# Two rules for dealing out feed-forward matmuls beside a top-k attention on one core

## The chip, the core and the metric

The kernel runs on one NeuronCore of a Trainium2 chip, as one program. The metric is the device time of that program in microseconds (us), the median of three runs. The core has five engines with an instruction stream each: TensorE (PE in the profile; its weight loads are PEld), VectorE (DVE), ScalarE (ACT), GpSimd (POOL) and SyncE (SP), which here issues the transfers.

## The reference

Attention with a top-k mask over 8 batches of 8 heads, 576 tokens and 64 elements a head, and then a gated feed-forward block over all 4608 tokens:

```python
scores = scale * np.matmul(q, k.transpose(0, 1, 3, 2))
kth = np.partition(scores, -32, axis=-1)[..., -32:-31]
scores = np.where(scores >= kth, scores, -1000000000.0)
attn = softmax(scores)                    # with 1e-9 added to the sum
x = attn @ v                              # as (4608, 512), heads side by side
out = (silu(x @ w_gate) * (x @ w_val)) @ w_out   # 512 -> 1536 -> 512
```

All inputs and outputs are float32.

## The kernel before

**Units.** The attention is cut into 160 units `(b, qt, hp)`: 8 batches, five tiles of queries, four pairs of heads. Within a batch the first 16 units hold 128 queries of two heads (double units, two rows of 576 scores for each partition); the last four, `qt == J`, hold the 64 left-over queries of both heads stacked in one tile (single units, one row). Unit 20b + 4qt + hp is the one with these three numbers, so units 16 to 19, 36 to 39, and so on are single.

**Stages of a unit.** TensorE makes the scores (L306, or L292 for a single unit) and ScalarE copies them out of PSUM (L311, L297). VectorE then finds the 32nd largest score of each row: four rounds of an eight-value maximum (L327) with three match-and-replace passes between (L331), and a comparison (L337). GpSimd adds the mask to the scores (`penalize`, L349). ScalarE takes the exponential and its sum (`weigh`, L358), VectorE the reciprocal (L370), and ScalarE scales (`normalize`, L373). TensorE transposes the weights (`turn`, L385; ScalarE copies them out, L386) and multiplies by v (`values`, L405 and L414; ScalarE copies the result into `xT`, L429). `prep` (L246) transposes k and q of a pair of heads once for each batch, on TensorE.

**The order of work.** There is no run-time scheduler: the main loop (L694) writes all instructions in order, and every engine keeps that order (the manual dependencies from L757 on see to it). Iteration n deals with several units at once: the top-k of unit n, the scores of n + 1, the penalty and exponential of n - 1, the scaling of n - 2, `turn` of n - 3, `values` of n - 4, and `prep` for unit n + 2 where that unit starts a pair. On TensorE an iteration is thus: turn, values, scores of the next unit, and then pieces of the feed-forward block.

**Pieces.** The feed-forward block works on 18 blocks of 256 tokens. `feed` (L454) is a generator that issues one block's matmuls in small steps and says what each one cost. A product of the gate or the value weights is two pieces of four matmuls, each of cost 1; there are twelve products, so 24 pieces. The down projection is seven quarter products of six matmuls, in pieces of three matmuls, each of cost 0.75: 14 pieces, 10.5 in sum. A block costs 34.5; the first, which is computed plainly, 36. A finished product puts its ScalarE work on a list, `on_act` (three instructions for a gate, L493 to L495; one copy for a value, L500), and GpSimd's work on `on_pool`; both are written into the streams at fixed places of the iteration (`flush`).

**Credit.** How many pieces an iteration may issue is set by `credit`. Each iteration adds 4.45 for a double unit and 2.25 for a single one, up to 8 (L714). `pieces(k)` (L667) issues up to k pieces as long as at least 1 is left, and an iteration calls it four times: 2 before the list for ScalarE is flushed and the scaling is written, then 1, 1 and up to 6. A block can begin only when `values` has filled all its tokens (`done`, L647); while none is ready, nothing is issued and the credit stays, up to 8. From unit 156 on the credit is 8 each time (L711). What is left after the loop is issued in one go (L751).

Of the kernel before, what the change touches and what calls it, by code (L numbers as in the profile page):

```python
# [27 lines left out]
def kernel(  # L28
# [40 lines left out]
    J = S // P  # L69
# [64 lines left out]
    def weights():  # L134
# [6 lines left out]
        for c in range(MC):  # L141
            for f in range(0, DM, WP):
                pieces.append((w_out[c * P : (c + 1) * P, f : f + WP], wo[:, c, f : f + WP]))
        pieces = [rounded(*p) for p in pieces]
        step = [0] * len(pieces)

        def upto(i, k):
# [51 lines left out]
    def rounding(n):  # L199
        for _ in range(n):  # L200
            next(weight, None)
# [9 lines left out]
    def load(i):  # L211
        b, hp = pairs[i]
        h = slice(2 * hp, 2 * hp + 2)
        kq = ld.tile([P, 2, J, 2, D], FP32, tag="kq", name="kq_in")
        kq_last = ld.tile([P, 2, D], FP32, tag="kql", name="kq_last")
        for n, src in ((0, k), (1, q)):
            queue = nc.scalar if n == 1 and i == 0 else nc.sync
            for hh in range(2):
                queue.dma_start(
                    kq[:, n, :, hh, :],  # L220
                    src[b, 2 * hp + hh, 0:JP].rearrange("(p j) d -> p j d", j=J),
                )
            queue.dma_start(
                kq_last[n * R : (n + 1) * R], src[b, h, JP:S].rearrange("h p d -> p h d")
            )
        raw[i] = (kq, kq_last)
# [42 lines left out]
    units = [(b, qt, hp) for b in range(B) for qt in range(J + 1) for hp in range(NHP)]  # L269
    state = {}  # L270

    def n_heads(qt):

        return 1 if qt == J else 2

    def scores(n):
        b, qt, hp = units[n]
        slab = preps[b * NHP + hp]
        sc = work.tile([P, 2 * S], FP32, tag="sc", name="sc", bufs=2)
        halves = [slice(0, D), slice(D, P)]  # L280
        half = S // 2

        def bank():
            return ps_t.tile([P, 512], FP32, tag="t", name="s")


        if qt == J:
            banks = [bank() for _ in range(2)]
            for i, ps in enumerate(banks):
                for d in halves:  # L290
                    k0 = R + i * half
                    nc.tensor.matmul(  # L292
                        ps[d, 0:half], slab[d, S + R : S + 2 * R], slab[d, k0 : k0 + half]
                    )
            yield
            for i, ps in enumerate(banks):
                nc.scalar.copy(sc[:, i * half : (i + 1) * half], ps[:, 0:half])  # L297
        else:
            q0 = S + 2 * R + qt * P
            banks = []  # L300
            for i in range(2):
                for hh, d in enumerate(halves):
                    ps = bank()
                    banks.append((i + 2 * hh, ps))
                    k0 = (1 - hh) * R + i * half
                    nc.tensor.matmul(  # L306
                        ps[:, 0:half], slab[d, q0 : q0 + P], slab[d, k0 : k0 + half]
                    )
            yield
            for i, ps in banks:  # L310
                nc.scalar.copy(sc[:, i * half : (i + 1) * half], ps[:, 0:half])  # L311
        state[n] = dict(sc=sc)

    def select(n):

        nh = n_heads(units[n][1])
        sc = state[n]["sc"]
        m = small.tile([P, 2, TOP_K], FP32, tag="m", name="m", bufs=2)
        heads = [slice(t * S, (t + 1) * S) for t in range(nh)]
        rest = work.tile([P, 2 * S], FP32, tag="rest", name="rest", bufs=1)  # L320
        e = work.tile([P, 2 * S], FP32, tag="e", name="e", bufs=4)
        state[n] |= dict(m=m, e=e, heads=heads)
        cur = sc
        rounds = TOP_K // 8
        for r in range(rounds):
            for t, hs in enumerate(heads):
                nc.vector.max(m[:, t, 8 * r : 8 * r + 8], cur[:, hs])  # L327
                yield
            if r < rounds - 1:
                for t, hs in enumerate(heads):  # L330
                    nc.vector.match_replace(  # L331
                        rest[:, hs], m[:, t, 8 * r : 8 * r + 8], cur[:, hs], LOWEST
                    )
                    yield
                cur = rest
        for t, hs in enumerate(heads):
            nc.vector.tensor_scalar(  # L337
                e[:, hs], sc[:, hs], m[:, t, TOP_K - 1 : TOP_K], FAR, ALU.is_lt, ALU.mult
            )

    def penalize(n):

        st = state[n]
        sc, m, e, heads = st.pop("sc"), st.pop("m"), st["e"], st["heads"]
        nh = len(heads)
        bias = small.tile([P, 2], FP32, tag="bias", name="bias")
        nc.gpsimd.tensor_scalar_mul(bias[:, 0:nh], m[:, 0:nh, 0], -scale)
        every = slice(0, nh * S)
        nc.gpsimd.tensor_tensor(e[:, every], e[:, every], sc[:, every], ALU.add)  # L349
        st["bias"] = bias  # L350
# [15 lines left out]
    def normalize(n):  # L366
        st = state[n]
        tot, e, heads = st.pop("tot"), st["e"], st.pop("heads")
        nh = len(heads)
        nc.vector.reciprocal(tot[:, 0:nh], tot[:, 0:nh])  # L370
        yield
        for t, hs in enumerate(heads):
            nc.scalar.mul(e[:, hs], e[:, hs], tot[:, t : t + 1])  # L373
# [76 lines left out]
    def flush(queue):  # L450
        while queue:
            queue.pop(0)()
# [186 lines left out]
    def piece():  # L639

        if len(on_act) > 1:
            flush(on_act)
        if len(on_pool) > 1:
            flush(on_pool)
        while True:
            if not current:
                if not todo or done.get(todo[0], 0) < NHP * BLK:  # L647
                    return 0
                flush(on_act)
                flush(on_pool)  # L650
                current.append(feed(todo.pop(0)))
            cost = next(current[0], 0)
            if cost == 0:
                current.pop()
                continue
            return cost

    def fetch(n):

        b, qt, hp = units[n]  # L660
        i = b * NHP + hp
        if qt == 0:
            yield from prep(i)
        if qt == J and i + NHP < len(pairs):
            load(i + NHP)

    def pieces(n):  # L667
        for _ in range(n):
            if credit[0] >= 1:
                credit[0] -= piece()  # L670

    def run(steps):
        for _ in steps:
            pass

    def finish_unit(n):
        values(n)
        b, qt, hp = units[n]
        if qt == J and b + 1 < B:
            load_v((b + 1) * NHP + hp)  # L680
# [8 lines left out]
    credit = [0.0]  # L689
    no = iter(())  # L690
    over = {}
    TURN, VALUES = 3, 4
    due = [0.0]
    for n in range(NU + VALUES):  # L694
        nh = n_heads(units[n][1]) if n < NU else 1
        topk = select(n) if n < NU else no
        over[n - 1] = normalize(n - 1) if 0 <= n - 1 < NU else no
        nxt = scores(n + 1) if n + 1 < NU else no
        ahead = fetch(n + 2) if n + 2 < NU else no
        norm = over.pop(n - 2, no)  # L700

        def dve(k, beside=True):

            for _ in range(k * nh):
                next(topk, None)
                due[0] += 5 / 11 if beside else 0
                if due[0] >= 1:
                    due[0] -= 1
                    rounding(1)

        if n >= NU - NHP:  # L711
            credit[0] = 8.0
        else:
            credit[0] = min(credit[0] + (4.45 if nh == 2 else 2.25), 8.0)  # L714
        flush(on_act)
        if 0 <= n - 1 < NU:
            penalize(n - 1)
        flush(on_pool)
        if 0 <= n - TURN < NU:
            run(turn(n - TURN))  # L720
        if n >= VALUES:
            finish_unit(n - VALUES)
        next(nxt, None)

        early[0]()
        if 0 <= n - 1 < NU:
            weigh(n - 1)
        run(nxt)

        dve(2, beside=False)  # L730
        if 2 <= n + 2 < NHP:
            load(n + 2)
        if n < NHP:
            load_v(n)
        pieces(2)
        flush(on_act)
        dve(1)
        dve(1)
        next(norm, None)
        run(norm)  # L740

        flush(on_pool)
        next(ahead, None)
        pieces(1)
        next(ahead, None)
        dve(1)
        pieces(1)
        dve(2)
        run(topk)
        pieces(6)  # L750
# [50 lines left out]
```

## Time and profile before

| | before |
|---|---|
| runs, us | 1870.55, 1870.92, 1871.88 |
| span of the profiled execution, us | 1870.2 |
| mean granted TensorE clock | 0.957 |
| PE busy, us (share) | 1715.9 (92%) |
| DVE busy, us (share) | 1632.2 (87%) |
| ACT busy, us (share) | 1210.1 (65%) |
| POOL busy, us (share) | 1023.4 (55%) |
| moved between HBM and core | 59.67 MB, mean 32 GB/s |

How to read it: busy time is summed over the whole span, start and end included. The ends of matmuls are modelled in the profile, so a busy PE says that it had something in hand, and not that it ran at its full rate. The page also cuts the span into 40 slices of 46.8 us and gives the busy share of each in tenths. A wait is put down to the instruction whose semaphore came last.

### The profile page before, as it was taken

Reading aid. Unit: us, or ns where it says so; the run is one execution under the profiler, and the core shown is the slowest. Engines: PE = TensorE matmul, PEld = TensorE weight load, DVE = VectorE, ACT = ScalarE, POOL = GpSimd, SP = SyncE. Lnnn points to the kernel's source line nnn. Section 1 sums busy time; section 2 is a strip of 40 time slices with the busy share of each in tenths; the row PEclk is TensorE's granted clock in tenths of the full one; section 3 lists DMA queues with packets and bytes.
Section 4 is the critical chain, followed back from the end, with each engine's and each line's share of the span. In section 5 each row is a group of like instructions: output and inputs, shape, how many; then the busy total and the mean of one; then the engine's idle time right before and its main releaser. Section 6 shows DMA issues by size and latency. Waiting matters only on the chain.

```text
span 1870.2 us, 30845 instructions
## 1 busy us (share of the span) xinstructions
PE 1715.9 (92%) x10756; PEld 1415.0 (76%) x10756; DVE 1632.2 (87%) x3477; ACT 1210.1 (65%) x3015; POOL 1023.4 (55%) x1007
## 2 busy tenths in 40 slices
PE   3447899899999999898999999989999999899998
PEld 2336658778888878787788887878888878787877
DVE  7999999998999989997999989999999989999300
ACT  5667667666757676765666676667666667676431
POOL 4666755645465646454455555555456545455534
PEclk7668999999999999999999999999999999999989
DMA  7332121000300021000200002000200001000000
GB/s 188 96 85 80 64 65 26 12 1 8 84 1 12 1 60 32 12 1 13 71 20 1 12 16 76 1 12 2 70 21 13 1 17 50 12 1 12 1 12 12
DMA packets 111259, 59.67 MB, mean 32 GB/s; under 512 B 89088, under 2 KB 97280, under 8 KB 111104
## 3 DMA queue, kind: packets, MB, share of 16 engines
q1 hardware_dynamic: 109904, 57.41, 11.6%
q8 instruction: 85, 1.39, 0.3%
q14 instruction: 70, 0.57, 0.1%
q10 hardware_dynamic: 1200, 0.30, 0.1%
HBM read 48.23 MB, written 9.44 MB: 31 GB/s over the span
## 4 chain that ended last, share of the span: by engine, by line
PE 80%; DVE 7%; ACT 4%; POOL 3%; issue 2%; DMA 0%; POOLq 0%; ACTq 0%; SPq 0%
PE f L468 39%; PE x_ps L554 8%; PE av L414 8%; PE etps L385 8%; PE s L306 6%; PE y_ps L554 5%; DVE m L327 3%; DVE rest L331 2%; PE s L292 2%; PE av L405 1%; ACT e L358 1%; PE kqps L261 1%; PE o_ps L514 1%; POOL e L349 1%; ACT sc L311 1%
## 5 line engine op out<-in xcount | busy, mean ns | idle before, releaser
L327 DVE MAX8 m<-rest 128x8 f32<-128x576 f32 x864 | 615.0, 746 | 2.2
L331 DVE MATCH_REPLACE8 rest<-m,rest 128x576 f32<-128x576 f32 x576 | 423.7, 742 | 0.0
L349 POOL TENSOR_TENSOR e<-e,sc 128x1152 f32<-128x1152 f32 (+1 forms) x160 | 382.7, 2392 | 59.5 <-DVE e L337 56.8
L468 PE MATMUL f<-xT,wg 128*128 128x256 f32 x1728 | 403.8, 384 | 0.0
L468 PE MATMUL f<-xT,wv 128*128 128x256 f32 x1728 | 397.9, 381 | 0.0
L468 PEld LDWEIGHTS f<-xT,wg 128*128 128x128 f32 x1728 | 323.7, 191 | 66.2 <-issue 23.9
L468 PEld LDWEIGHTS f<-xT,wv 128*128 128x128 f32 x1728 | 324.4, 190 | 55.6 <-issue 13.5
L496 POOL TENSOR_TENSOR h<-h,half_g 128x512 f32<-128x512 f32 x108 | 137.9, 1276 | 372.3 <-ACT h L495 360.6
L327 DVE MAX8 m<-sc 128x8 f32<-128x576 f32 x288 | 205.3, 749 | 122.7 <-ACT sc L297 71.1
L385 PE MATMUL etps<-ident,e 128*128 128x128 f32 (+1 forms) x1312 | 191.0, 291 | 122.3 <-issue 38.5
L358 ACT ACTIVATE e<-e,bias 128x576 f32<-128x576 f32 x288 | 222.0, 776 | 94.3 <-POOL e L349 94.3
L385 PEld LDWEIGHTS etps<-ident,e 128*128 128x128 f32 (+1 forms) x1312 | 161.9, 150 | 153.6 <-issue 45.4
L386 ACT COPY et<-etps 128x512 f32<-128x512 f32 (+1 forms) x448 | 185.1, 484 | 127.1 <-PE etps L385 125.6
L501 POOL TENSOR_TENSOR h<-h,val 128x512 f32<-128x512 f32 x108 | 139.4, 1291 | 159.4 <-ACT val L500 159.4
L373 ACT ACTIVATE e<-e,tot 128x576 f32<-128x576 f32 x288 | 211.6, 788 | 5.6 <-DVE tot L370 5.6
L331 DVE MATCH_REPLACE8 rest<-m,sc 128x576 f32<-128x576 f32 x288 | 211.8, 742 | 0.0
L414 PE MATMUL av<-et,v 128*64 128x128 f32 (+1 forms) x2560 | 175.7, 284 | 0.0
L337 DVE TENSOR_SCALAR e<-sc,m 128x576 f32<-128x576 f32 x288 | 172.6, 636 | 3.4
L306 PE MATMUL s<-kqT 64*128 64x288 f32 x1024 | 169.8, 447 | 4.2 <-ACT kqT L266 3.8
L311 ACT COPY sc<-s 128x288 f32<-128x288 f32 x512 | 163.8, 403 | 1.7 <-PE s L306 1.7
L493 ACT ACTIVATE h<-f 128x512 f32<-128x512 f32 x108 | 65.2, 604 | 150.7 <-PE f L468 150.7
L414 PEld LDWEIGHTS av<-et,v 128*64 128x64 f32 x2560 | 138.6, 146 | 23.4 <-issue 7.7
(71 smaller groups left out, 2042.0 us busy)
## 6 DMA issues: line engine op xcount, KB each, us to landing
kq_in<-in_k_dram SPq DMA_DIRECT2D x64, 128.0 KB, 2.8
v<-in_v_dram SPq DMA_DIRECT2D x32, 256.0 KB, 2.9
kq_in<-in_q_dram SPq DMA_DIRECT2D x62, 128.0 KB, 2.9
w<-in_moe_w_gate_dram SPq DMA_DIRECT2D x24, 256.0 KB, 2.7
w<-in_moe_w_val_dram SPq DMA_DIRECT2D x24, 256.0 KB, 2.7
w<-in_moe_w_out_dram SPq DMA_DIRECT2D x24, 256.0 KB, 2.6
out_dram<-o SPq DMA_DIRECT2D x40, 128.0 KB, 2.4
out_dram<-o SPq DMA_DIRECT2D x16, 256.0 KB, 2.4
```

Source lines behind the costliest of these rows:

```text
L306: nc.tensor.matmul(ps[:, 0:half], slab[d, q0 : q0 + P], slab[d, k0 : k0 + half])
L311: nc.scalar.copy(sc[:, i * half : (i + 1) * half], ps[:, 0:half])
L327: nc.vector.max(m[:, t, 8 * r : 8 * r + 8], cur[:, hs])
L331: nc.vector.match_replace(rest[:, hs], m[:, t, 8 * r : 8 * r + 8], cur[:, hs], LOWEST)
L349: nc.gpsimd.tensor_tensor(e[:, every], e[:, every], sc[:, every], ALU.add)
L358: nc.scalar.activation(e[:, hs], e[:, hs], AF.Exp, bias=bias[:, t : t + 1], scale=scale, accum_out=tot[:, t : t + 1],)
L373: nc.scalar.mul(e[:, hs], e[:, hs], tot[:, t : t + 1])
L385: nc.tensor.transpose(ps[0:kl, c * P : (c + 1) * P], e[:, k0 : k0 + kl], ident[:])
L386: nc.scalar.copy(et[0:kl, c0 : c0 + cn, :], ps[0:kl, 0 : cn * P].rearrange("p (c j) -> p c j", c=cn),)
L414: nc.tensor.matmul(av[hh * R : (hh + 1) * R, 0:ql], v_last[:, hh, :] if c == J else vt[:, hh, c, :], moving, start=last and c == 0, stop=c ...
L468: nc.tensor.matmul(ps[:, i, :], w[:, kc, m * P : (m + 1) * P], x[:, kc, :], start=(kc == 0), stop=(kc == KC - 1),)
L554: nc.tensor.matmul(ps, lhsT, T[i][m], start=m == 0, stop=m == MQ - 1)
```

## The change

From iteration 28 on, the credit that an iteration gets is no longer a constant for each kind of unit. A new function, `share(n)`, starts from 6.4 for a double unit (3.2 for a single one) and takes off what TensorE has to do in the same iteration for attention, in units of one piece: 0.7 for scores, 0.6 for the transposes, 0.7 for the product with v, each halved where the unit concerned is a single one, and 0.6 where a `prep` falls into the iteration. A plain double iteration so gets 4.4, the single ones 0.90 to 1.55. The second part is the limit: credit is kept only up to `share(n) + 1`, where it was up to 8. The first 28 iterations, the last four units and the issue at the end follow the old rule. No instruction is added or taken away on any engine; they are issued in another order.

```diff
+    def share(n):
+        others = 0.0
+        for m, cost in ((n + 1, 0.7), (n - TURN, 0.6), (n - VALUES, 0.7)):
+            others += cost * (0.5 if units[m][1] == J else 1)
+        if units[n + 2][1] == 0:
+            others += 0.6
+        return 6.4 * n_heads(units[n][1]) / 2 - others
...
     TURN, VALUES = 3, 4
+    HEAD = 28
...
         if n >= NU - NHP:
             credit[0] = 8.0
+        elif n < HEAD:
+            credit[0] = min(credit[0] + (4.45 if nh == 2 else 2.25), 8.0)
         else:
-            credit[0] = min(credit[0] + (4.45 if nh == 2 else 2.25), 8.0)
+            credit[0] = min(credit[0] + share(n), share(n) + 1)
```

## Prediction, made before the changed kernel ran

> **What bounds the kernel now.** I read the page first: busy shares and slices. PE has most to do, and its row stands at 8 or 9 tenths from the fourth slice on, but so does DVE's, so the averages don't decide it.
>
> ```profile
> PE 1715.9 (92%) x10756; PEld 1415.0 (76%) x10756; DVE 1632.2 (87%) x3477; ACT 1210.1 (65%) x3015; POOL 1023.4 (55%) x1007
> ...
> PE   3447899899999999898999999989999999899998
> ...
> DVE  7999999998999989997999989999999989999300
> ```
>
> The view of waits, kept to DVE and then PE after 330 us, decides it:
>
> ```profile
> DVE m L327 <- ACT sc L297: 71.1, 23, 11.0
> DVE m L327 <- ACT sc L311: 47.1, 35, 2.4
> ```
>
> ```profile
> PE etps L385 <- issue: 23.0, 12, 3.0
> PE etps L385 <- ACT e L373: 16.3, 9, 2.1
> ```
>
> The top-k waits 118 us for scores, at the start of 58 units; PE waits some 43 us, nearly all at the first transpose of an iteration. So PE is late and DVE waits, over most of the kernel.
>
> Next, what a piece costs. The chain of waits gives groups of feed-forward matmuls (four matmuls, a piece, are eight records), and the timeline of the end, where nothing else is on PE, two pieces (16 records) at a time:
>
> ```profile
> 302.00 7.11 PE f L468 x32
> 312.51 8.83 PE f L468 x40
> 858.00 14.01 PE f L468 x64
> ```
>
> ```profile
> 1820.74 3.62 PE L468 MATMUL f<-xT,wv 128*128 128x256 f32 x16
> 1824.20 3.62 PE L468 MATMUL f<-xT,wg 128*128 128x256 f32 x16
> ```
>
> From 1820.74 to 1824.20, 3.46 us for two pieces: 1.73 us a piece of cost 1; quarters follow each other every 2.59 us, the same per cost. From 302.00 to 312.51 a plain double iteration with four pieces takes 10.51 us, so turn, values and scores take 10.51 - 6.92 = 3.6. A top-k of two rows needs 10.57 us (unit starts 359.58 and 370.15 in the timeline), of one row 6.27.
>
> Now I set this sum beside each interval from one unit's scores to the next's on PE. Most agree within 0.1 us. The windows of those that don't (columns: PE, PEld, DVE, ACT and POOL busy, PE clock, DMA):
>
> ```profile
> 364.90:373.60 8.70, 5.69 (x40) 4.61 (x37) 8.70 (x20) 6.00 (x16) 2.81 (x2) 0.70 0.00 0
> 733.60:745.00 11.40, 11.40 (x75) 9.64 (x73) 11.40 (x26) 7.24 (x19) 6.10 (x10) 1.00 0.01 2
> 745.00:753.60 8.60, 6.63 (x51) 4.96 (x49) 7.06 (x16) 6.39 (x17) 7.17 (x5) 1.00 0.00 0
> 753.60:762.30 8.70, 5.69 (x41) 4.63 (x37) 8.70 (x21) 6.00 (x16) 1.51 (x3) 0.72 0.17 62
> ```
>
> The second is full (4.5 pieces). The third has 1.5 pieces, the first and fourth none, because no block was ready and the credit could not be spent: PE had 3.6 us of work in 8.7. Busy PE of 5.7 there is slow work, at a clock of 0.70, not more work. The eight pieces saved up then come at once (858.00 is such a burst) and DVE waits up to 11 us. A lost PE microsecond in such a hole is lost for good, since PE is the bound before and after it.
>
> [...] in a single unit:
>
> ```profile
> 657.01 3.72 PE L468 MATMUL f<-xT,wv 128*128 128x256 f32 x16
> 660.77 0.58 ACT L500 COPY val<-f 128x512 f32<-128x512 f32 x1 [1.67 <-PE f L468]
> 661.25 1.44 ACT L373 ACTIVATE e<-e,tot 128x576 f32<-128x576 f32 x2
> ```
>
> The scaling (L373) stands behind the copy of a product that PE has just ended, and the next transposes, at 662.13, need the scaling: PE stops for about 1.8 us though its data had long been ready. [...]
>
> **The change part by part.** *The amount of work* is the same on every engine; what can move is PE's lost time. Between the scores of unit 28 (344.7) and of unit 156 (1716.9), the sum of (interval - work) is 65.3 us over the 29 intervals that lose more than 0.3:
> - entry hole, iterations 29 to 31: 13.9
> - holes and their bursts at 65 to 67 (8.5), 73 and 74 (5.2), 109 and 110 (5.7), 145 to 147 (8.3), 153 and 154 (5.2): 32.9
> - single units 56, 57, 76 to 78, 97, 136, 137: 13.3
> - six others, 0.5 to 1.6 each: 5.3
>
> *Removed.* I followed credit and `done` through both rules, iteration by iteration. Shares for a batch sum to 16 x 6.4 + 4 x 3.2 - 38.4 = 76.8; a batch brings 2.25 blocks x 34.5 = 77.6 (before: 80.2). So the new rule always has a ready block after unit 31; the holes vanish: 32.9 us saved. The entry hole stays, as block 2 is not complete.
>
> *Single units* get one or two pieces for two or three. By the rule seen above, a product that ends last in an iteration costs 1.8 (value) or 2.8 (gate: three ACT instructions), 1.1 for a gate with one piece behind it, some 0.5 where a `prep` covers it. The new order has: iteration 36 value 1.8; 76 gate 2.8; 97 and 117 gate and one piece, 1.1 each; 78, 98, 118 0.5 each: 8.4, and 1.5 for iterations with one piece, whose ACT chain (copies of the transposes, exponentials, scores) takes about 5.5 us against 5.2 on PE. Sum 9.9 against 13.3 (bounds: 5, if half of it hides, and 20, if all four units of a batch lose 0.8 us each).
>
> *Double units* get 4 or 5 pieces as before, at least two after the scaling, 3.5 us, which hides evacuation and scaling; more often now a gate ends last in an iteration, and the 20 or so of these cost the 0.2 us that such intervals show today. Others: 5.3 + 4.4, call it 10 (bounds 5, as now, and 26, rival 1).
>
> *Queues.* POOL's products move with the pieces. SP's stores move among the loads, but loads are written two units before use, 20 us, against a landing of 2.9; hidden. VectorE's stream is unchanged. A ready engine waits for nothing new: the added queueing is only scaling behind evacuation, priced above.
>
> *The end.* Pieces done before unit 156's share: 561.5 before, 554.5 after. Seven (12.1 us) move behind it, where PE is the bound as well: neutral in itself. But 2.25 of them fall into iteration 160, which has none now, between transposes that wait for ACT:
>
> ```profile
> 1794.21 0.77 PE L385 MATMUL etps<-ident,e 128*128 128x128 f32 x5 [2.07 <-ACT e L373]
> 1797.25 1.33 PE L385 MATMUL etps<-ident,e 128*128 128x128 f32 x5 [0.98 <-ACT e L373]
> ```
>
> From 1790.56 to 1801.44 there are 10.9 us for 5.7 of work; I take 3 of the 5.2 as filled (bounds 0 and 5).
>
> *Sum*: lost before 65.3; after 13.9 + 9.9 + 10 = 33.8; saved 31.5 + 3 = 34.5. Against the profiled span, 1870.2 - 34.5 = 1835.7; the three runs' median is 0.7 above that span: **1836 us**. DVE is no floor: from unit 28 on it needs 104 x 10.57 + 24 x 6.27 = 1250 us against the 1372 it takes now.
>
> **The rivals.**
> 1. *New stalls eat half.* With the holes gone, PE meets ACT's and POOL's queues oftener: the down projection waits for GpSimd's sums, evacuations delay score copies. For: six such losses of 0.5 to 1.6 today, of unknown rule; single units get thinner. Against: long full stretches today lose under 0.1 an iteration. At 0.13 us more on each of 124 iterations, 16 us: 1852.
> 2. *All of it comes out.* Singles and others lose almost nothing, the end fills wholly: 10 to 15 us more, 1823. For: batch 1's single iterations today (2.25 pieces of quarters) lose nothing. Against: gates do end there.
> 3. *Backlog, slower.* The seven pieces add 12.1 us after the top-k, and the middle doesn't get shorter, because DVE or the ACT chain sets its pace: 1870.9 + 12.1 - 3 = 1880. It decides only if new waits exceed what the holes gave, over 0.4 us on each of 124 iterations. Against: DVE waits today in 58 units.
> 4. *Nothing happens*, since a block's arrival sets the pace anyway. Against: blocks would be waiting in all iterations after 31.
>
> **How the numbers follow.** No change that this kernel can tell is 0.2%, 3.7 us. Chances: forecast 0.68 (1826 to 1846), rival 1 0.15 (1846 to 1866), rival 2 0.10 (below 1826), rival 3 0.05, rival 4 0.02. The range 1822 to 1856 takes the forecast, most of rival 2 and half of rival 1: about 0.85. Faster by over 0.2%: 0.93; within: 0.02; slower: 0.05.
>
> **What would show it.** In the changed profile: no interval of scores with PE clock near 0.7 after 382 us; DVE's waits for L297 and L311 down from 118 us to about 75, those over 4 us only after unit 156; PE's waits at L385 after 382 us cut by about half; PE busy lower, as the slow work in holes goes; last DVE instruction near 1734, 43.6 us earlier than now (31.5 saved before the end, and the 12.1 of the pieces that move behind it). Wrong if the holes come back elsewhere, if PE waits for POOL in the down projection, or if unit 156's scores come later than 1680.

## The result, and the profile after

The changed kernel takes 1845.37 us (median of four runs, 1843.96 to 1846.87) against 1870.83 for the kernel before: ratio 0.9863, 95% interval 0.9848 to 0.9878, that is 25.5 us less. Run again beside the later experiments it took 1845.83 (ratio 0.9876, 0.9856 to 0.9896). The forecast was 1836, the range 1822 to 1856.

The page of the changed kernel, busy shares and slices:

```profile
span 1843.6 us, 30858 instructions
...
PE 1708.1 (93%) x10756; PEld 1409.2 (76%) x10756; DVE 1623.5 (88%) x3477; ACT 1208.6 (66%) x3015; POOL 1026.2 (56%) x1007
...
PE   3447899999999989999999999999999999999998
...
DVE  7999999999999979997999989998999989998400
```

PE's row has almost no 8 left after the entry, and DVE ends its last comparison earlier (1745.3 us, before 1777.5). The times that the text gives for scores and for this comparison count, as in the prediction, from the first busy instruction, 0.24 us after the zero of the timelines. The waits after 330 us, DVE's and then PE's:

```profile
DVE m L327 <- ACT sc L297: 58.3, 14, 10.6
DVE m L327 <- ACT sc L311: 36.9, 29, 2.2
```

```profile
PE etps L385 <- issue: 11.5, 8, 3.0
PE etps L385 <- ACT e L373: 9.6, 7, 4.6
PE kqps L253 <- ACT sc L311: 2.5, 2, 1.6
```

DVE's two waits went from 118 to 95 us, PE's at the first transpose from 39 to 21. And the stretches in windows, from the scores of one unit to those of the next (columns: PE, PEld, DVE, ACT and POOL busy, PE clock, DMA share, GB/s). The first is the entry hole, the next two are units 66 to 68, where the kernel before had starved; the last three are intervals in single units:

```profile
365.00:373.60 8.60, 5.59 (x39) 4.58 (x36) 8.60 (x19) 6.00 (x16) 2.81 (x2) 0.70 0.00 0
...
737.50:748.80 11.30, 11.30 (x75) 9.55 (x73) 11.30 (x24) 5.91 (x16) 11.00 (x13) 1.00 0.01 1
748.80:760.20 11.40, 11.40 (x77) 9.65 (x73) 11.32 (x26) 7.24 (x19) 5.94 (x9) 1.00 0.00 1
649.00:661.80 12.80, 8.17 (x53) 6.19 (x49) 4.72 (x10) 5.72 (x14) 7.75 (x10) 0.87 0.02 4
861.60:872.60 11.00, 8.60 (x57) 6.54 (x53) 6.51 (x12) 6.93 (x16) 4.38 (x6) 0.89 0.02 4
1508.30:1516.40 8.10, 6.28 (x56) 4.47 (x50) 6.52 (x14) 5.41 (x17) 5.08 (x7) 0.93 0.45 101
```

The holes are gone: 11.3 and 11.4 us are full, at 4.5 pieces. The entry hole stands as it did. What is new is that some single units have become expensive: 12.8 us for 6.1 of work from unit 57's scores to unit 58's.

**The ledger.** The prediction's sum (interval minus 1.73 us a piece and the attention's own work, itself 1.17 for scores, 1.05 for turn, 1.33 for values, less for single units, 1.08 for a prep) can be made for every kernel that ran. It is the time that PE lost between the scores of units 28 and 156, small losses included, and it is the reading on which the rest stands. "Entry" is the hole at iterations 28 to 31; "double" holds the later holes; an interval counts as single when the pieces in it come from a single unit's iteration.

| kernel | median, us | ratio to before (interval) | entry | double | single | lost, us |
|---|---|---|---|---|---|---|
| before | 1870.83 | | 14.0 | 42.4 | 13.0 | 69.4 |
| changed | 1845.37 | 0.9863 (0.9848 to 0.9878) | 13.9 | 12.4 | 21.5 | 47.8 |
| e1 | 1853.19 | 0.9931 (0.9909 to 0.9953) | 12.9 | 17.0 | 25.4 | 55.3 |
| e2 | 1865.65 | 0.9987 (0.9974 to 1.0001) | 12.6 | 32.2 | 15.9 | 60.7 |
| e3 | 1853.78 | 0.9927 (0.9900 to 0.9954) | 14.0 | 16.9 | 25.4 | 56.3 |
| e4 | 1835.49 | 0.9836 (0.9815 to 0.9858) | 11.6 | 12.5 | 14.2 | 38.3 |
| e5 | 1838.87 | 0.9825 (0.9803 to 0.9847) | 14.1 | 11.6 | 15.7 | 41.4 |
| e8 | 1836.76 | 0.9814 (0.9796 to 0.9832) | 11.6 | 17.1 | 8.7 | 37.4 |
| e9 | 1840.07 | 0.9833 (0.9815 to 0.9850) | 11.6 | 14.4 | 17.7 | 43.7 |
| e10 | 1832.15 | 0.9798 (0.9783 to 0.9813) | 12.5 | 12.5 | 9.6 | 34.6 |
| e11, changed again | 1845.83 | 0.9876 (0.9856 to 0.9896) | 12.5 | 11.9 | 22.0 | 46.4 |

The ratios are to runs of the kernel before on the same chip; its medians there were 1868.4 (e1 to e4), 1871.6 (e5 to e9) and 1869.5 (e10, e11). Up to iteration 35 the changed kernel, its repeat e11, e4 and e10 issue the same instructions in the same order, and still their entry columns run from 11.6 to 13.9: differences of some 2 us in the last column are not to be read as a kernel's doing. The ledger closes: 69.4 - 47.8 = 21.6 us saved up to unit 156, and from there to the end the changed kernel needs 2.6 us more, though 4.5 more pieces (7.8 us) are left to it, so 5.2 are saved there; 26.8 in all, against 26.6 between the two spans.

### The profile page after: what moved, and what is told of

Read it like the earlier page. It is cut to its first block, busy times and chain, and to the rows that moved or that the text cites. A ratio compares the mean times of both kernels' runs of the same rounds, so it can differ in the third digit from the quotient of the medians.

```text
span 1843.6 us, 30858 instructions
## 1 busy us (share of the span) xinstructions
PE 1708.1 (93%) x10756; PEld 1409.2 (76%) x10756; DVE 1623.5 (88%) x3477; ACT 1208.6 (66%) x3015; POOL 1026.2 (56%) x1007
## 3 DMA queue, kind: packets, MB, share of 16 engines
q1 hardware_dynamic: 109904, 57.41, 11.8%
## 4 chain that ended last, share of the span: by engine, by line
PE 83%; DVE 6%; ACT 3%; POOL 3%; issue 2%; DMA 0%; POOLq 0%; ACTq 0%
PE f L468 39%; PE x_ps L554 9%; PE av L414 8%; PE etps L385 7%; PE s L306 7%; PE y_ps L554 6%; DVE m L327 2%; DVE rest L331 2%; PE s L292 2%; PE av L405 1%; PE o_ps L514 1%; PE kqps L261 1%; POOL e L349 1%; ACT e L358 1%; DVE e L337 1%
## 5 line engine op out<-in xcount | busy, mean ns | idle before, releaser
L349 POOL TENSOR_TENSOR e<-e,sc 128x1152 f32<-128x1152 f32 (+1 forms) x160 | 382.7, 2392 | 67.2 <-DVE e L337 61.7
L385 PE MATMUL etps<-ident,e 128*128 128x128 f32 (+1 forms) x1312 | 186.7, 287 | 104.3 <-POOL size L126 36.2
L385 PEld LDWEIGHTS etps<-ident,e 128*128 128x128 f32 (+1 forms) x1312 | 159.6, 147 | 133.1 <-POOL size L126 39.0
L337 DVE TENSOR_SCALAR e<-sc,m 128x576 f32<-128x576 f32 x288 | 165.4, 610 | 3.4
```

The costliest lines, as they stand in the source:

```text
L337: nc.vector.tensor_scalar(e[:, hs], sc[:, hs], m[:, t, TOP_K - 1 : TOP_K], FAR, ALU.is_lt, ALU.mult)
L385: nc.tensor.transpose(ps[0:kl, c * P : (c + 1) * P], e[:, k0 : k0 + kl], ident[:])
```

## The experiments

**Which half of the change does it.** e1 takes the share and keeps the old limit of 8; e2 keeps the old rates and takes the new limit; e3 takes neither, only a slower constant. (Three edits of one line are set together; the comments name the run.)

```diff
-            credit[0] = min(credit[0] + share(n), share(n) + 1)
+            credit[0] = min(credit[0] + share(n), 8.0)                             # e1
+            rate = 4.45 if nh == 2 else 2.25                                       # e2
+            credit[0] = min(credit[0] + rate, rate + 1)                            # e2
+            credit[0] = min(credit[0] + (4.27 if nh == 2 else 2.13), 8.0)          # e3
```

> Half of the change: the new share, but credit is kept up to 8 as before. Theory (time is TensorE's lost time; what counts is that no iteration after the entry hole goes without pieces): the order has no empty iteration after unit 31, so the time stays within 5 us of the changed kernel, 1840 to 1850, and the limit alone is worth little. Rival (the limit does the work, by keeping bursts out): bursts return and the time goes back towards 1860 or more.

> The other half: the old rates 4.45 and 2.25 from unit 28 on, but at most one piece carried over. Theory: TensorE still overtakes the blocks, with empty iterations at units 66, 110 and 146, each some 5 us lost, and single units about as in the kernel before: 1850 to 1857, between the two kernels. Rival (the limit does the work): 1840 to 1846.

> Neither part, but a slower constant: 4.27 for double and 2.13 for single units from unit 28 on (the same sum for a batch as the share), credit kept up to 8. Theory (rate alone closes the holes): one thin iteration, at unit 66, is left; single units get two pieces, and gates that end there cost ScalarE's queue as before: 1843 to 1852. Rival (it matters that the share takes off what attention does in the same iteration): 1856 or more.

Measured: e1 1853.2, e2 1865.7, e3 1853.8. All three are slower than expected of the theory; e1 and e3 by 2 to 3 us beyond their ranges, e2 by 9. e1 and e3 lie between what theory and rival expected, nearer to the theory, and can't be told apart; that both are faster than e2 fits the theory. With the old rate holes are back whatever the limit, as the windows of e2 show (the second holds no piece):

```profile
742.10:753.70 11.60, 10.49 (x69) 8.35 (x67) 9.37 (x18) 6.66 (x18) 8.08 (x9) 1.00 0.00 1
753.70:762.10 8.40, 5.39 (x43) 4.21 (x37) 8.40 (x19) 6.00 (x16) 3.08 (x4) 0.81 0.17 64
762.10:774.40 12.30, 12.30 (x77) 10.34 (x75) 12.30 (x29) 8.19 (x20) 5.83 (x5) 0.99 0.00 0
```

The burst after the hole is smaller (five pieces, not eight), but an iteration without pieces still loses 4.0 to 4.9 us at units 67, 111 and 147 (before 3.3 to 5.1): bursts had been a sign and not the loss. The old holes at units 75 and 155 shrink to 1.6 us each, so double units lose 32.2 and not 42.4; 3 us of that come back behind unit 156, where e2 has the same pieces left as the kernel before and takes longer. Why e2 missed its range by 9 us is not explained beyond that. The limit alone brings nothing that can be told from no change (the interval takes in 1). The lower rate alone (e3) brings some 14 us of the 25, and whether it is shaped by neighbours (e1) or flat (e3) makes no difference at the old limit; a flat rate with the new limit was not run. On top of the share the limit is worth more than e1's expectation had it ("worth little"): 7.8 us between e1 and the changed kernel, 7.5 in the ledger, of which 3.9 in single and 4.6 in double units, less 1.0 at the entry. These losses seem to depend on which piece happens to end where; that the limit is good for them as such is not shown.

**What costs 6.7 us at unit 56.** In e4 the last call for pieces in iteration 55 may issue two and not six, so that the first piece of quarter 2 goes to iteration 56.

```diff
-        pieces(6)
+        pieces(6 if n != 55 else 2)
```

> The changed kernel, but iteration 55 leaves its last piece (the first of quarter 2 of block 4) to iteration 56. With that piece GpSimd's sums of the down projection come ahead of unit 55's penalty. Theory (GpSimd's fixed order is what costs 6.7 us between the scores of units 57 and 58): that interval loses under 1.5 us and the time falls by 5 to 7 us, to about 1839. Rival (the loss comes from too little TensorE work in single units, whatever GpSimd does): the interval still loses 5 us or more and the time is unchanged.

Measured: 1835.5, and the interval in question loses 0.04 us. The changed kernel's timeline shows why it was dear. Unit 55's comparison ends at 642.05, and its penalty (L349) begins at 651.66:

```profile
640.15 1.90 DVE L337 TENSOR_SCALAR e<-sc,m 128x576 f32<-128x576 f32 x2
...
645.82 0.58 ACT L588 COPY p<-y_ps 128x512 f32<-128x512 f32 x1 [2.00 <-PE y_ps L554]
...
646.48 0.73 POOL L540 TENSOR_TENSOR p<-p 128x256 f32<-128x256 f32 x1 [1.86 <-ACT p L588]
...
647.98 1.48 POOL L540 TENSOR_TENSOR p<-p,p 128x512 f32<-128x512 f32 x1
...
649.43 2.08 POOL L602 TENSOR_TENSOR h<-h,xT 128x256 f32<-128x256 f32 x3
...
651.66 2.61 POOL L349 TENSOR_TENSOR e<-e,sc 128x1152 f32<-128x1152 f32 x1
...
654.30 0.77 ACT L358 ACTIVATE e<-e,bias 128x576 f32<-128x576 f32 x1 [4.68 <-POOL e L349]
...
657.84 1.99 PE L385 MATMUL etps<-ident,e 128*128 128x128 f32 x9 [4.62 <-ACT e L373]
```

GpSimd's stream has the down projection's sums first, because the piece that calls for them was issued at the end of iteration 55, and they wait for a quarter that PE ends only at 645.8 (the copy L588 stands between). Behind them stands the penalty; behind it, on ScalarE, the exponential, the copies of the next scores and the scaling; and PE waits for the scaling. In e4 the same penalty begins 1.4 us after the comparison ends, and not 9.6:

```profile
637.66 1.90 DVE L337 TENSOR_SCALAR e<-sc,m 128x576 f32<-128x576 f32 x2
...
640.98 2.63 POOL L349 TENSOR_TENSOR e<-e,sc 128x1152 f32<-128x1152 f32 x1
...
648.84 0.73 POOL L540 TENSOR_TENSOR p<-p 128x256 f32<-128x256 f32 x1 [4.54 <-ACT p L588]
...
650.55 1.15 PE L385 MATMUL etps<-ident,e 128*128 128x128 f32 x9
```

e4's interval holds 0.75 more of a piece (1.3 us), too little to hide 6.7, so the rival falls. Not all of e4's gain is this one place: the interval behind it now loses 1.4 us, the later pieces shifted too, and iterations 76 and 77 lose 2.1 us there against 4.5. The time fell by 9.9 us, where 5 to 7 were expected; 2.3 of the 9.5 in the ledger stand at the entry, ahead of the edit.

**ScalarE's order.** e5 writes the scaling ahead of the evacuation in single units.

```diff
         pieces(2)
-        flush(on_act)
+        single = HEAD <= n < NU - NHP and nh == 1
+        if not single:
+            flush(on_act)
...
         run(norm)
+        if single:
+            flush(on_act)
```

> The changed kernel, but in single units from 28 to 155 the scaling (L373) is written ahead of the evacuation of what the first two pieces finished. Theory (ScalarE's fixed order costs TensorE the pause at single units 36, 76, 97 and 117): those intervals, which lose 1.8, 4.1, 1.1 and 1.1 us, lose under 0.5 each; units 56 and 139, where GpSimd is the cause, keep their 6.7 and 3.0; the time falls by 6 to 8 us. Rival (the evacuation that now comes later holds PSUM and GpSimd up as long): no change, within 2 us of the changed kernel.

Measured: 1838.9. Of the four intervals, those of iterations 76, 97 and 117 lose 0.04 us each now; 36 still loses 1.0, what a lone piece there leaves uncovered. Iteration 56 keeps its 6.7, 139 keeps 2.1 of 2.9. The gain came out as forecast, but not wholly by the forecast's route: where the pause at iteration 76 went, iteration 77, with one piece, now loses 2.3 where it lost 0.4. The chain of waits moves to the penalty there:

```profile
871.49 0.78 ACT L358 ACTIVATE e<-e,bias 128x576 f32<-128x576 f32 x1 [1.64 <-POOL e L349]
...
873.17 1.45 ACT L373 ACTIVATE e<-e,tot 128x576 f32<-128x576 f32 x2
...
874.05 1.38 PE L385 MATMUL etps<-ident,e 128*128 128x128 f32 x9 [1.87 <-POOL e L349]
```

**Both at once.** e8 adds to e5 a general rule: from unit 28 on no iteration ends with the piece that brings the sums. e10 adds to e5 only e4's line. The lines that matter, the places between them left out:

```diff
+                    sums_next[0] = i == 6 and m == MQ - 1     # in quarter, before the yield
...
+            sums_next[0] = False                              # in piece, before the next step
...
-            if credit[0] >= 1:
+            if credit[0] >= 1 and not (hold and sums_next[0]):
...
-        pieces(6)
+        pieces(6, hold=n >= HEAD)                             # e8
+        pieces(6 if n != 55 else 2)                           # e10
```

> Both orders mended at once: the scaling first in single units, and from unit 28 on no iteration ends with the piece that brings GpSimd's sums ahead of the next penalty (it goes to the next iteration). Theory: single units lose 8 us or less over 28 to 155, of 21.5 in the changed kernel; lost time in all 30 to 36 us of 48; time 1830 to 1836. Rival (losses only move to double units): time as in the changed kernel, 1842 to 1848.

> The changed kernel with both small mends that cost double units nothing: scaling first in single units, and iteration 55 leaves its last piece to 56. Theory (the two causes are separate, so their gains add): single units lose some 9 us of the 21.5, double units stay at 12, all lost time 33 to 36; 12 to 15 us below the changed kernel run beside it, which gives 1828 to 1833. Rival (they share a cause): as e4 or e5 alone, 5 to 9 us below.

> The changed kernel itself, unaltered, on the chip on which the version with both mends runs: 1842 to 1848 by both theories.

Measured: e8 1836.8, just above its range; e10 1832.2, 13.7 below e11, the changed kernel on the same chip. Single units lose 8.7 and 9.6 us. In e8 the rival was partly right: double units lose 17.1 instead of 12.4, because a held piece brings the sums late and the down projection's last quarter waits for them. PE's waits in e8 (where these lines stand one and two places lower in the file) and in e10:

```profile
PE x_ps L555 <- POOL h L604: 5.6, 5, 1.4
```

```profile
PE x_ps L554 <- POOL h L602: 0.4, 1, 0.4
```

e10 has the lowest time of all: 0.9798 of the kernel before (0.9783 to 0.9813), an interval that overlaps e8's.

**Is moving pieces to the end neutral?** e9 starts the share from 6.3.

```diff
-        return 6.4 * n_heads(units[n][1]) / 2 - others
+        return 6.3 * n_heads(units[n][1]) / 2 - others
```

> One size: the share starts from 6.3 for a double unit, not 6.4. By unit 155 it has issued 11.5 pieces fewer, 19.9 us of TensorE, which go behind the last double unit. Theory (TensorE is the bound before and behind, so moving work to the end is neutral): within 6 us of the changed kernel. Rival (the backlog adds to the end, and VectorE sets the pace before): some 20 us slower, 1860 or more.

Measured: 1840.1, within the theory's 6 us and if anything faster. Unit 156's scores come at 1664.4 and not 1687.7, with 11 pieces (19.0 us) more behind them. From there to the end e9 takes 17.1 us longer than the changed kernel, no more than these pieces cost, and PE is full at the start of that stretch:

```profile
1664.40:1719.40 55.00, 55.00 (x318) 46.11 (x315) 28.22 (x57) 26.89 (x62) 28.55 (x31) 1.00 0.04 11
```

A backlog of this size costs no time of its own. The rival that was to make the change slower is refuted.

## Why the prediction was right, and where its size was off

- *PE is the bound, and its lost time is what can move:* right. With one set of costs, span less lost time comes to 1793.7 to 1796.8 us in the nine executions at the lower rate, and to 1800.8 and 1803.8 in the two at the old one (before, e2), whose ends take longer; e10 and e11 differ by 11.8 us in the ledger and by 12.2 in span.
- *Holes, 32.9 us, vanish; the entry hole stays:* right. No interval after 382 us has a clock near 0.7, and double units lose 30 us less. e2 brings holes back, and the time with them.
- *Other losses in double units, 10 us:* about right, 9.4 measured. Intervals over 0.3 us, the prediction's count, lose 6.5; the intervals of 0.2 us, for which it set 4.4 aside, are fourteen and not some twenty, 2.9 us. The old kernel had eight of these too, 1.7 us, which the 65.3 leaves out.
- *Single units, 9.9 us:* the step that failed; by the same count 21.7. (Its listed parts add up to 8.3 and not 8.4, which changes nothing.) Three terms make the difference. At iterations 56 and 139, 6.7 and 2.9 against 0: the prediction said that GpSimd's products move with the pieces and that a ready engine waits for nothing new, and had rival 1 for it only in general. It never asked what stands ahead of the penalty on GpSimd when the sums of the down projection fall at a single unit. For iteration 56, the larger part, e4 shows it; for 139, e5 with the scaling first alone still loses 2.1, and e8, which also holds such a piece back, 0.1. At iteration 76, 4.1 against 2.8: the pause was foreseen, the slow restart behind it was not (below). At 96 and 116, 0.9 and 1.0 against the 0.4 of a share of 1.5: a lone half product doesn't cover ScalarE's chain.
- *The end, 3 us of 5.2:* 5.2 measured; of PE's two waits there, 2.07 and 0.98 us, one of 0.99 is left.
- *The signs.* Rightly foreseen: PE's waits at L385 after 382 us cut by half or more (32.0 to 13.8), PE busy lower by 7.8 us. Missed: the last comparison at 1745 (1734 forecast), DVE's waits at 95 us (75 forecast), with waits over 4 us before units 57, 77, 97 and 117, and unit 156's scores at 1687.7, past the 1680 that was named as a sign of error. The two times are late mainly because 21.6 us and not 31.5 were saved ahead of them. For unit 156's scores a slip of counting made the forecast some 4 us too early as well: seven pieces were taken to lie behind unit 156's scores, but the scores are issued before the pieces of iteration 155, and only 4.5 do. The sum of the forecast does not hang on it. Nor does a misreading of DVE's longest wait, put down to a burst: the 11.0 us stand at unit 159, in the end; the burst at 858 us made DVE wait 8.8.
- *Rival 1* (new stalls eat half; 1852) was half right in its kind, with 8 us and not 16.
- *The sum.* By the profiled spans the forecast missed by 7.9 us: single units came out 11.9 worse, double units 1.8 and the end 2.2 better. That the total is nearer than its worst term is luck.

What stays open: the changed kernel still loses 47.8 us and e10 34.6, of which some 12.5 is the entry, for which block 2 would have to be complete earlier; that was not tried, and some 12 are spread over the double units. No version without single units' thin iterations was tried either.

## What to carry to other kernels

When two engines are both near 90% busy, find the one whose idle time is lost, and keep a ledger for it stage by stage: interval minus known work names each loss in microseconds, and it closes on the span. A rate set a few per cent too high was worse here than one set a little too low (0.9987 of the kernel before in e2, 0.9833 in e9), as what was left could be done where the same engine is the bound anyway: e9's 11 pieces took 17.1 us there. And before moving work in a hand-written order, ask on every engine that the moved piece feeds what it will now stand ahead of: two instructions in the wrong order on GpSimd and ScalarE cost more here (13.7 us from e11 to e10) than the limit on credit brought (7.8 us from e1 to the changed kernel).

## What the runs showed of the hardware that was not expected

A short pause of PE can cost more than its length. In the changed kernel, after 4.62 us of waiting, the same nine transposes and sixteen products take 1.99 and 1.94 us, where one unit later they take 1.15 and 1.09:

```profile
657.84 1.99 PE L385 MATMUL etps<-ident,e 128*128 128x128 f32 x9 [4.62 <-ACT e L373]
...
660.18 1.94 PE L414 MATMUL av<-et,v 128*64 128x128 f32 x16
...
665.87 1.15 PE L385 MATMUL etps<-ident,e 128*128 128x128 f32 x9
...
667.17 1.09 PE L414 MATMUL av<-et,v 128*64 128x128 f32 x16
```

The pause itself is 4.62 of the 6.7 us that the interval loses. The granted clock was 1.00 in it, 0.60 over the work that follows, and 1.00 over the same work one unit later (columns as above):

```profile
653.20:657.80 4.60, 0.01 (x1) 0.00 (x0) 0.83 (x2) 3.47 (x10) 1.68 (x2) 1.00 0.00 0
657.80:662.10 4.30, 4.25 (x29) 3.49 (x29) 4.16 (x10) 1.99 (x4) 1.87 (x4) 0.60 0.02 4
665.90:668.20 2.30, 2.30 (x30) 2.01 (x28) 2.27 (x5) 1.24 (x3) 0.00 (x0) 1.00 0.03 7
```

Two pauses of one length need not cost the same. At iteration 76 both kernels pause for 2.40 us behind the gate that ends last. Afterwards the sixteen products take 1.98 us in the changed kernel, whose interval loses 4.1 us, and 1.09 us in the kernel before, which loses 2.8:

```profile
869.07 1.53 PE L385 MATMUL etps<-ident,e 128*128 128x128 f32 x9 [2.40 <-issue]
...
870.96 1.98 PE L414 MATMUL av<-et,v 128*64 128x128 f32 x16
872.87 1.52 PE L292 MATMUL s<-kqT 64*64 64x288 f32 x8
```

```profile
881.41 1.38 PE L385 MATMUL etps<-ident,e 128*128 128x128 f32 x9 [2.40 <-issue]
...
882.94 1.09 PE L414 MATMUL av<-et,v 128*64 128x128 f32 x16
883.97 1.19 PE L292 MATMUL s<-kqT 64*64 64x288 f32 x8
```

And the windows of the pause and of what follows it, two of the changed kernel and then two of the one before:

```profile
866.70:869.10 2.40, 0.03 (x1) 0.06 (x1) 2.33 (x7) 2.39 (x5) 0.71 (x1) 1.00 0.00 0
870.90:872.90 2.00, 2.00 (x19) 1.61 (x18) 0.64 (x1) 0.33 (x1) 2.00 (x3) 0.50 0.04 8
```

```profile
879.00:881.40 2.40, 0.01 (x1) 0.02 (x1) 2.33 (x7) 2.35 (x5) 0.68 (x1) 1.00 0.00 0
881.40:884.00 2.60, 2.59 (x29) 2.08 (x29) 2.34 (x3) 1.91 (x4) 2.16 (x3) 1.00 0.00 0
```

In the changed kernel the clock was 0.50 over the products, in the kernel before 1.00 from the first transpose on. From there to the next scores PE takes 3.80 against 2.56 us, and that is why the prediction's 2.8 us, measured in the old kernel, became 4.1. Such a pause can't be priced by its length alone; what decided between the two is not shown here.
